# Decode attention with a cached K and V: K loaded through the DMA's transposing crossbar, V and weights moved to a second queue, scores laid out by key group

## The chip, the cores, the metric

One core of a Trainium2 chip (trn2). The metric is the device time of one execution, in microseconds (us). Most executions of a kernel agree within 0.3%; where a run fell in a slower state it is said. Engines: PE is TensorE, DVE is VectorE, ACT is ScalarE, POOL is GpSimd, SP is SyncE, which issues loads. PEld is TensorE's loading of weights, a q after an engine's name (SPq) is its instruction queue, and L488 is line 488 of the kernel. K and V are the cached keys and values; the two measuring kernels below ran once each, so their state is unknown.

## The reference, cut

Two identical layers, run one after the other on 4 batch rows with one token each. Each layer is grouped attention over a cache (32 query heads, 8 K/V heads, 4096 keys, head size 128), then a gated MLP (a GLU).

```python
def _A_ref(x, k_cache, v_cache, wq, wo):          # x: 4 x 1 x 512
    q = (x @ wq).reshape(B, 1, 32, 128).transpose(0, 2, 1, 3)
    k = repeat(k_cache, 4, axis=1)                # 4 x 8 x 4096 x 128 before repeat
    v = repeat(v_cache, 4, axis=1)
    p = softmax(einsum("bhqd,bhkd->bhqk", q, k) * 128 ** -0.5)
    return einsum("bhqk,bhkd->bhqd", p, v)... @ wo
# reference: x += A(norm(x)); x += B(norm(x)); and both once more, same weights, same caches
```

Both layers use the same K and V. The kernel reads K once for a row and keeps it until layer 2 has used it, and reads V twice: 32 MiB of K, 64 MiB of V, 13.25 MiB of weights.

## The kernel before

A small planner in the kernel gives each operation an engine and an order, and gives each K or V tile one of the slots of a ring in SBUF. Everything is loaded by SyncE, in one order. A tile is half of a K or V head (512 KiB), and the ring has 22 slots. K arrives as it lies in memory, keys on partitions; VectorE turns it in 32 x 32 blocks of pairs, in place.

```python
    NS = 22                                        # ring slots of 512 KiB
    ...
    def load_piece(src, q):
        t = _Tile(src)
        def fn(e):
            return e.dma_start(
                ring[t.slot], t.src.rearrange("(p t) d -> p (t d)", p=P)[:, q * TS:(q + 1) * TS])
        S.load(t, fn, P * TS * 2)                  # SyncE's queue
        return t
    ...
    def transpose_k(b, g, q, prio):                # VectorE, 64 times
            v = ring[t.slot].bitcast(dt.int32)
            return e.transpose(v, v)
    ...
    def scores(b, s, u, prio):                     # rows by head
            for nn in range(NQ):
                for gi in range(4):
                        kt = ring[t.slot].rearrange("p (t bb j r) -> p t bb j r", bb=2, j=32, r=2)
                        return e.matmul(
                            bank[32 * gi:32 * gi + 16, :], lhsT=qbd[u % NQB][:, gi, nn, :],
                            rhs=kt[:, :, nn // 2, :, nn % 2], start=nn == 0, stop=nn == NQ - 1)
    ...                                            # softmax; the probabilities are transposed twice
    # load order for row b: V (layer 2 of row b-1, heads 0..2), K(b), V (layer 1), V (layer 2 of b-1, heads 3..7)
```

The score matmuls read columns 4 bytes apart. A K slot is free only when layer 2's scores have read it, and these need the whole of layer 1 for that row.

## Time and profile before

| | before |
|---|---|
| median of 2 runs | 348.98 us (348.31 to 349.64) |
| span of the profiled run | 344.2 us |
| bytes moved | 115.3 MB, all but a little on one queue |
| TensorE / VectorE / ScalarE busy | 222.9 / 138.4 / 52.8 us |
| K transposes on VectorE | 64, 75.8 us |
| score matmuls | 512, four at a time in 0.43 us at half clock |

The page of the kernel before. The rows with 40 digits or numbers cut the span into 40 slices of 8.6 us: DMA is the busy share of the 16 DMA engines in tenths, GB/s what they moved. The last line is a DMA queue: packets, MB, share of the engines' time.

```profile
span 344.2 us, 11881 instructions
...
DMA  7999999999489999998599999957999999977800
GB/s 264 375 401 409 408 345 365 409 401 377 192 275 405 410 407 372 374 381 320 172 393 409 409 368 347 404 179 280 334 416 407 410 354 382 343 284 256 356 5 2
...
q1 hardware_dynamic: 36816, 114.57, 88.1%
```

In the slices in which nothing holds it up, the queue runs at 401 to 416 GB/s; at 410 GB/s the bytes are 281 us. The rest of the span is visible as low slices: 192, 172, 179 and the last two.

The chain of waits of the same kernel, by engine and then by line (share of the span):

```profile
DMA 40%; PE 27%; issue 14%; DVE 10%; SPq 7%; POOLq 0%; ACT 0%; DVEq 0%
DMA ring<-in_A_v_cache_dram 31%; PE S_ps L488 7%; PE O_ps L571 6%; PE M_ps L298 6%; PE Y_ps L298 5%; DMA wd<-in_B_w_down_dram 5%; SPq L331 5%; DVE ring L475 4%; DMA wo<-in_A_wo_dram 3%; PE G_ps L298 2%; SPq L347 2%; DVE ml L504 2%; DMA ring<-in_A_k_cache_dram 2%; PE PT_ps L298 1%; DVE qbd L466 1%
```

Loads lead; VectorE's K transposes (DVE ring) are 4% of it. In the costliest groups (columns: line, engine, operation, out<-in, shape, count | busy us, mean ns | idle before it and its main cause) they look much larger:

```profile
L571 PE MATMUL O_ps<-pt_sb,ring 128*128 128x4 bf16 x2048 | 67.2, 167 | 39.5 <-DMA ring<-in_A_v_cache_dram 31.6
...
L475 DVE STREAM_TRANSPOSE ring<-ring 128x1024 int32<-128x1024 int32 x64 | 75.8, 1216 | 8.6 <-DMA ring<-in_A_k_cache_dram 8.2
L488 PE MATMUL S_ps<-ring,qbd 128*16 128x512 bf16 x512 | 55.7, 590 | 12.0 <-DVE ring L475 12.0
```

75.8 us of work, of which 4% of the span stood in the way. One of the dips, in windows of 4 us (busy us of each engine with instruction counts, clock, DMA share, GB/s), and one undisturbed window:

```profile
core 0: us, PE busy (x) PEld busy (x) DVE busy (x) ACT busy (x) POOL busy (x), PEclk, DMA share, GB/s
160.00:164.00 4.00, 3.10 (x102) 2.99 (x101) 0.58 (x2) 0.18 (x1) 0.54 (x1) 0.50 0.70 271
164.00:168.00 4.00, 4.00 (x60) 1.48 (x60) 1.26 (x3) 0.18 (x1) 0.00 (x0) 0.50 0.24 67
...
256.00:260.00 4.00, 2.00 (x21) 0.43 (x18) 3.93 (x7) 0.00 (x0) 0.00 (x0) 0.50 1.03 414
```

At 164 us the DMA rate drops to 67 GB/s: the ring is full of K tiles that wait for the scores of layer 2. SyncE's waits show it: four times loads waited for a score matmul, once for 14 us:

```profile
engine line waited for: us in total, times, longest us
SPq L190 <- PE S_ps L488: 38.9, 4, 14.0
```

These scores, in order of time (start, duration, engine, line, operation, count):

```profile
164.02 1.89 PE L488 MATMUL S_ps<-ring,qbd 128*16 128x512 bf16 x16
```

16 matmuls of 512 columns in 1.89 us, four column groups at a time. By their starts, each four begin 0.43 us after the four before (the granted clock was half in this window, 0.50).

### The profile page before, as it was taken

Reading aid. Unit: us, or ns where it says so; the run is one execution under the profiler, and the core shown is the slowest. Engines: PE = TensorE matmul, PEld = TensorE weight load, DVE = VectorE, ACT = ScalarE, POOL = GpSimd, SP = SyncE. Lnnn points to the kernel's source line nnn. Section 1 sums busy time; section 2 is a strip of 40 time slices with the busy share of each in tenths; the row PEclk is TensorE's granted clock in tenths of the full one; section 3 lists DMA queues with packets and bytes.
Section 4 is the critical chain, followed back from the end, with each engine's and each line's share of the span. In section 5 each row is a group of like instructions: output and inputs, shape, how many; then the busy total and the mean of one; then the engine's idle time right before and its main releaser. Section 6 shows DMA issues by size and latency. Waiting matters only on the chain.

```text
span 344.2 us, 11881 instructions
## 1 busy us (share of the span) xinstructions
PE 222.9 (65%) x5426; PEld 171.2 (50%) x5426; DVE 138.4 (40%) x341; ACT 52.8 (15%) x128; POOL 10.6 (3%) x38
## 2 busy tenths in 40 slices
PE   1332861265877578676874697596784787777876
PEld 1202551155635147676352376493452586762865
DVE  3777620000189951101699620011899400016111
ACT  1003030000033203000241130000323110003300
POOL 6000000000000000000000000000000000000001
PEclk9999999999995555555655555555655555558555
DMA  7999999999489999998599999957999999977800
GB/s 264 375 401 409 408 345 365 409 401 377 192 275 405 410 407 372 374 381 320 172 393 409 409 368 347 404 179 280 334 416 407 410 354 382 343 284 256 356 5 2
DMA packets 36897, 115.32 MB, mean 335 GB/s; under 512 B 3312, under 2 KB 9200, under 8 KB 36848
## 3 DMA queue, kind: packets, MB, share of 16 engines
q1 hardware_dynamic: 36816, 114.57, 88.1%
q8 instruction: 42, 0.69, 0.8%
q14 instruction: 7, 0.06, 0.0%
q10 hardware_dynamic: 32, 0.00, 0.0%
HBM read 114.56 MB, written 0.00 MB: 333 GB/s over the span
## 4 chain that ended last, share of the span: by engine, by line
DMA 40%; PE 27%; issue 14%; DVE 10%; SPq 7%; POOLq 0%; ACT 0%; DVEq 0%
DMA ring<-in_A_v_cache_dram 31%; PE S_ps L488 7%; PE O_ps L571 6%; PE M_ps L298 6%; PE Y_ps L298 5%; DMA wd<-in_B_w_down_dram 5%; SPq L331 5%; DVE ring L475 4%; DMA wo<-in_A_wo_dram 3%; PE G_ps L298 2%; SPq L347 2%; DVE ml L504 2%; DMA ring<-in_A_k_cache_dram 2%; PE PT_ps L298 1%; DVE qbd L466 1%
## 5 line engine op out<-in xcount | busy, mean ns | idle before, releaser
L571 PE MATMUL O_ps<-pt_sb,ring 128*128 128x4 bf16 x2048 | 67.2, 167 | 39.5 <-DMA ring<-in_A_v_cache_dram 31.6
L571 PEld LDWEIGHTS O_ps<-pt_sb,ring 128*128 128x128 bf16 x2048 | 63.7, 105 | 48.0 <-DMA ring<-in_A_v_cache_dram 20.3
L475 DVE STREAM_TRANSPOSE ring<-ring 128x1024 int32<-128x1024 int32 x64 | 75.8, 1216 | 8.6 <-DMA ring<-in_A_k_cache_dram 8.2
L488 PE MATMUL S_ps<-ring,qbd 128*16 128x512 bf16 x512 | 55.7, 590 | 12.0 <-DVE ring L475 12.0
L528 ACT ACTIVATE p_sb<-S_ps,cols 128x512 bf16<-128x512 f32 x32 | 24.6, 773 | 92.3 <-DVE cols L523 92.3
L504 DVE TENSOR_REDUCE ml<-S_ps 128x1 f32<-128x512 f32 x32 | 21.6, 674 | 38.1 <-PE S_ps L488 38.1
L580 DVE TENSOR_TENSOR oT<-O_ps,winv 128x12 bf16<-128x12 f32 (+2 forms) x29 | 4.9, 169 | 68.9 <-PE O_ps L571 68.7
L488 PEld LDWEIGHTS S_ps<-ring,qbd 128*16 128x16 bf16 x512 | 13.5, 111 | 34.0 <-issue 17.6
L298 PE MATMUL Y_ps<-oT,wo 128*128 128x1 bf16 (+1 forms) x640 | 20.4, 166 | 9.2 <-DVE oT L580 5.7
L298 PEld LDWEIGHTS Y_ps<-oT,wo 128*128 128x128 bf16 x640 | 18.7, 104 | 11.5 <-DVE oT L580 7.0
L298 PE MATMUL PT_ps<-ident_b,p_sb 128*128 128x64 bf16 x128 | 11.0, 228 | 18.6 <-ACT p_sb L528 18.4
L298 PEld LDWEIGHTS PT_ps<-ident_b,p_sb 128*128 128x128 bf16 x128 | 7.0, 116 | 26.4 <-ACT p_sb L528 24.5
L298 PE MATMUL M_ps<-xT,wq 128*128 128x1 bf16 x512 | 15.4, 165 | 6.7 <-issue 4.1
L298 PEld LDWEIGHTS M_ps<-xT,wq 128*128 128x128 bf16 x512 | 14.5, 104 | 7.5 <-issue 4.3
L298 PE MATMUL M_ps<-dsel,cols 128*128 128x16 f32 x64 | 15.1, 355 | 2.7 <-DVE dsel L553 2.7
L437 POOL TENSOR_TENSOR cols<-cols 128x1 f32<-128x1 f32 (+1 forms) x10 | 6.4, 640 | 325.0 <-issue 217.4
L433 DVE TENSOR_SCALAR cols<-G_ps 128x1 f32<-128x1 f32 (+1 forms) x10 | 1.6, 158 | 35.7 <-PE G_ps L298 35.7
L298 PEld LDWEIGHTS M_ps<-dsel,cols 128*128 128x128 f32 x64 | 13.7, 298 | 3.4 <-DVE dsel L553 2.8
L426 ACT ACTIVATE gs<-xj,cols 128x4 f32<-128x4 f32 x8 | 2.4, 297 | 81.6 <-DVE cols L424 81.6
L547 ACT ACTIVATE pt_sb<-PT_ps 128x512 bf16<-128x512 f32 x16 | 9.6, 597 | 22.4 <-PE PT_ps L298 22.4
L298 PE MATMUL G_ps<-cols 128*128 128x1 f32 (+1 forms) x40 | 11.4, 354 | 2.4 <-DVE cols L403 0.9
L536 ACT ACTIVATE p_sb<-PT_ps 128x512 bf16<-128x512 f32 x16 | 9.6, 597 | 12.3 <-PE PT_ps L298 12.3
(73 smaller groups left out, 151.2 us busy)
## 6 DMA issues: line engine op xcount, KB each, us to landing
ring<-in_A_v_cache_dram SPq DMA_DIRECT2D x128, 512.0 KB, 7.5
ring<-in_A_k_cache_dram SPq DMA_DIRECT2D x64, 512.0 KB, 11.9
wq<-in_A_wq_dram SPq DMA_DIRECT2D x4, 1024.0 KB, 12.4
wo<-in_A_wo_dram SPq DMA_DIRECT2D x4, 1024.0 KB, 11.1
wg<-in_B_w_gate_dram SPq DMA_DIRECT2D x1, 1792.0 KB, 13.8
wu<-in_B_w_up_dram SPq DMA_DIRECT2D x1, 1792.0 KB, 11.8
wd<-in_B_w_down_dram SPq DMA_DIRECT2D x1, 1792.0 KB, 16.4
x<-in_A_x_dram SPq DMA_DIRECT2D x1, 4.0 KB, 1.6
```

Source lines behind the costliest of these rows:

```text
L298: return lambda e: e.matmul(o, lhsT=l, rhs=r, start=start, stop=stop)
L331: return e.dma_start(ring[t.slot], t.src.rearrange("(p t) d -> p (t d)", p=P)[:, q * TS:(q + 1) * TS])
L347: S.put("sp", lambda e: e.dma_start(o, i), 0.55, 0, writes=[key], dma=key, nbytes=nbytes)
L437: "pool", lambda e: e.tensor_tensor(rs, vpe[:, 0:nb], mhalf[:, 0:nb], ALU.pow), 0.6, prio,
L475: return e.transpose(v, v)
L488: return e.matmul(bank[32 * gi:32 * gi + 16, :], lhsT=qbd[u % NQB][:, gi, nn, :], rhs=kt[:, :, nn // 2, :, nn % 2], start=nn == 0, stop=nn ...
L504: "dve", lambda e, q=q: e.tensor_reduce(ml[:, q:q + 1], S_ps[banks[q]][:], AX.X, ALU.max, negate=True), 0.65,
L528: "act", lambda e, q=q: e.activation(p_sb[:, 4 * q:4 * q + 4, :].rearrange("p c x -> p (c x)"), S_ps[banks[q]][:], ACTF.Exp, bias=nbias, s ...
L536: "act", lambda e: e.activation(pt1.rearrange("p c g a h -> p (c g a h)"), PT_ps[:], ACTF.Copy), 0.65, prio,
L547: "act", lambda e: e.activation(pt_sb[pi][:].rearrange("p q c g h -> p (q c g h)"), PT_ps[:], ACTF.Copy), 0.65,
L571: return e.matmul(O_ps[:, gi * R:(gi + 1) * R], lhsT=ring[tile.slot][:, (t % HT) * DH:(t % HT + 1) * DH], rhs=pt_sb[pi][:, t % 4, t // 4, ...
L580: "dve", lambda e: e.tensor_tensor(o, O_ps[:, c0:c1], winv[pi][:, c0:c1], ALU.mult), 0.2, prio - 1.5,
```

## The change

Its intent: take the K transposes off VectorE by letting the DMA's crossbar turn K on its way in; with whole K heads turned, let each score matmul contract the full head size against a diagonal query block, with the rows of a score tile by key group instead of by head, which drops the spreading of q and the second transposition of the probabilities. Crossbar loads go on SyncE's queue, V and weights on GpSimd's. Tiles are whole heads (1 MiB) in 11 slots. The GLU's gate and up matmuls are split in four, so that a reciprocal root (rstd, GpSimd's power) runs under them. Core of the diff, cut:

```diff
-    NS = 22
+    NS = 11
@@ loads
-        def fn(e):
-            return e.dma_start(
-                ring[t.slot], t.src.rearrange("(p t) d -> p (t d)", p=P)[:, q * TS:(q + 1) * TS]
-            )
+    def load_k(b, g):
+        t = K[b, g] = _Tile(A_k[b, g])
+        S.load(t, "sp", lambda e, t=t: e.dma_start_transpose(ring[t.slot], t.src), P * TS * 2, 0.6, 3.9)
+    def load_v(l, b, g, parts=1):
+            S.load(
+                t, "pool", lambda e, t=t, i=i: e.dma_start(ring[t.slot][:, i * n:(i + 1) * n], t.src[:, i * n:(i + 1) * n]),
+                P * n * 2, 1.0,
+            )
-    def load_w(key, o, i, nbytes):
+    def load_w(key, o, i, nbytes, eng="pool"):
@@ scores: no transposes on VectorE
-                            bank[32 * gi:32 * gi + 16, :], lhsT=qbd[u % NQB][:, gi, nn, :],
-                            rhs=kt[:, :, nn // 2, :, nn % 2], start=nn == 0, stop=nn == NQ - 1,
+                            S_ps[u % 2][32 * j:32 * j + 16, q, :], lhsT=qd[:, 16 * g:16 * g + 16],
+                            rhs=ring[t.slot].rearrange("d (p t) -> d t p", t=T)[:, t0:t0 + 4, :],
+                            start=g == 0, stop=g == 3,
@@ GLU: gate and up in four pieces each, rstd after the second
+            for f0, f1 in ((0, 3), (3, 6), (6, 10), (10, NF)):
```

The number 3.9 is the planner's own: it takes SyncE as blocked for 3.9 us by each crossbar load of 1 MiB, and plans the bytes at the plain rate. V needs keys by `(p t)`, so the scores must read K's columns `t` apart: 32 columns, 64 bytes.

## The prediction

> **What bounds the kernel now.** The loads. The page counts 115.3 MB in a span of 344.2 us. In undisturbed slices (the page's second part) the queue moves 405 to 411 GB/s; at 410 the bytes alone are 281 us. The other 63 us are gaps. By the table of 4 us windows: the start (4 us), the tail after the last load (324 to 344, 19 us), one dip per batch row, near 86-100, 160-172, 222-244 and 296-316 (about 9, 10, 14, 10 us); the rest is scattered. Each dip is one dependency: K tiles hold their ring slots until layer 2's scores have read them, which needs the whole chain last V tile, output projection, GLU, q projection, q spread, scores. In row 1 it ran from about 144 to 166 us (timeline). From one layer-2 score to the next (93.0, 164.0, 237.4, about 309) it is some 72 us, of which a row's 24 MiB are 61.4 us at 410 GB/s. VectorE's K transposes are 75.8 us busy (64 of 1.2 us), but only 3.6% (12 us) of the chain of waits: mostly hidden behind loads.
>
> **Removed.** The stream transposes; q spread (16 small matmuls and 0.43 us on VectorE per unit); the second transposition of the probabilities (16 matmuls, a 0.60 us ACT copy). Scores keep 512 matmuls of 512 columns (0.43 us per four in the cold clock), but start, and release, per K tile. On the dip's chain I count 2 to 3 us saved per row, some 10 us in all; in the first stage, where 84.5 us were used for bytes worth 75, 4 to 5 us.
>
> **Added.** (a) K through the crossbar. The new planner itself blocks SyncE 3.9 us per MiB (269 GB/s) and fills the rest with V, 2:1, so 8 K + 4 V take 31.2 us against 30.8 for plain loads: free, if the crossbar doesn't also use up the engines. The Trainium skill (DMA: Bandwidth & Descriptors, "Latency and other measured facts") gives 261 GB/s for a bad layout, about 350-400 for a contiguous one; K is contiguous. Estimate from that page: at 350, 32 MiB cost 14 us more; at 261 with nothing beside it, over 40. No trace here shows it yet. (b) GpSimd's queue also holds the rstd powers of the chain (0.54 us each): loads wait behind them and they behind loads. (c) A ring of 11 slots of 1 MiB leaves three, not six, for V while K is held, and less cover (7 MiB, not 8): 1 to 3 us per row. (d) Scores read K at a 64-byte stride; the skill (Advanced Engine Details and Errata, "Memory Cachelines") says changing the line at every access costs. At the half clock I expect little.
>
> **Sum.** 349 - 5 (start) - 10 (chain) - 6 (less VectorE and PE work in the V stages) + 7 (transposition, mostly filled) + 0 to 5 (GpSimd, ring) = 335 to 340. I predict 337 us, 80% range 316 to 364; faster 0.57, same 0.21, slower 0.22.
>
> **Checks.** Right: VectorE busy near 60 us; K tiles landing every 3.9 us while total GB/s stays near 400; one dip per row, 2 to 3 us shorter; period 67 to 70 us. Wrong: 270-330 GB/s throughout the K stages with engines full (crossbar-bound, slower); GpSimd's power waiting on loads; scores clearly above 0.43 us per four; V stages below 380 GB/s with PE waiting for V (three slots too few).

## The result, and the profile after

458.32 us (458.16 to 458.47, 2 runs) against 348.98 us: 31% slower, ratio 1.313 (1.302 to 1.324). A ratio here and below is the mean time of one kernel's fast runs over that of the other's of the same rounds, so not quite the ratio of the medians that are quoted. The predicted 337 us and its range of 316 to 364 missed it widely.

The page of the changed kernel, slices of 11.4 us:

```profile
span 456.0 us, 10567 instructions
...
DMA  8999978999999795999799995999799969985800
GB/s 252 370 311 243 230 161 333 323 366 307 192 292 262 123 226 199 373 366 228 195 302 211 239 76 195 382 360 220 202 328 212 276 122 405 358 303 201 357 4 2
...
q0 software_dynamic: 13120, 81.01, 49.6%
q1 hardware_dynamic: 132128, 33.56, 45.0%
```

The engines are busy nearly all the time (DMA row) and yet many slices move only 120 to 250 GB/s, and one 76. K's queue (q1) moved 33.56 MB in 132128 packets, 254 bytes each, and took 45% of the engines' time; V's and the weights' (q0) moved 81 MB in 13120 packets in 49.6%. Before, all 114.57 MB needed 36816 packets.

The chain of waits:

```profile
PE 32%; DMA 30%; SPq 20%; issue 13%; DVE 2%; ACT 1%; POOL 1%; DVEq 0%; ACTq 0%; POOLq 0%
SPq L315 19%; DMA ring<-in_A_v_cache_dram 13%; PE S_ps L443 12%; DMA ring<-in_A_k_cache_dram 12%; PE O_ps L509 6%; DMA wd<-in_B_w_down_dram 6%; PE M_ps L286 5%; PE Y_ps L286 5%; PE G_ps L286 3%; ACT p_sb L471 1%; DVE cols L457 1%; PE S_ps L286 1%; POOL ring L322 0%; POOL wo L327 0%; DVE oT L518 0%
```

SPq L315 is SyncE's sequencer at the line that issues the crossbar loads: 19% of the span it is held there. Score matmuls (L443) are 12%. The groups:

```profile
L443 PE MATMUL S_ps<-ring,q1d 128*16 128x512 bf16 x256 | 59.7, 1025 | 90.9 <-DMA ring<-in_A_k_cache_dram 86.8
...
L443 PE MATMUL S_ps<-ring,q2d 128*16 128x512 bf16 x256 | 57.2, 1031 | 0.4 <-issue 0.4
```

The score matmuls take 1025 ns each where they took 590, 116.9 us in all instead of 55.7, and those of layer 1 wait 86.8 us for K. In order of time, 48 of layer 2's in one go:

```profile
218.10 10.45 PE L443 MATMUL S_ps<-ring,q2d 128*16 128x512 bf16 x48
```

48 in 10.45 us are 0.87 us for four, where it was 0.43. Windows of 4 us (columns as before) in the K stage of the third row:

```profile
256.00:260.00 4.00, 0.00 (x0) 0.00 (x0) 0.00 (x0) 0.00 (x0) 0.00 (x0) 0.50 1.29 258
260.00:264.00 4.00, 0.00 (x0) 0.00 (x0) 0.00 (x0) 0.00 (x0) 0.00 (x0) 0.50 1.32 57
264.00:268.00 4.00, 0.00 (x0) 0.00 (x0) 0.00 (x0) 0.00 (x0) 0.00 (x0) 0.50 1.31 43
268.00:272.00 4.00, 1.28 (x8) 0.11 (x8) 0.00 (x0) 0.00 (x0) 0.00 (x0) 0.50 1.25 38
```

This is the strangest thing in the trace: from 260 to 272 us the DMA engines count as more than fully busy and move 38 to 57 GB/s. The trace's packet records show whose time this is. K's queue alone makes 1.19 to 1.25 of the busy share: its 256-byte packets took 283 to 321 ns each on average, where they took 18 from 240 to 244 us, with no V under way. V's packets of 8 KiB took 312 to 314 ns (their median in the whole run is 309), but only 11 to 20 of them went in 4 us. SyncE's crossbar loads (columns: duration of the issue, min/median/max):

```profile
engine op xcount: duration ns min/median/max, first and last start us, forms
L315 SPq DMA_TRANSPOSE ring<-in_A_k_cache_dram x32: 3881/5082/30418, 1.2 to 350.7; - x32
```

An issue takes 3.9 us at best, as the planner thought, 5.1 us typically and 30 us at worst. From one layer-2 score to the next it is 101, 104 and 91 us, where it was 71.0, 73.4 and 71.0.

VectorE did what was meant: 54.6 us busy instead of 138.4.

### The profile page after: what moved, and what is told of

It is laid out like the page before. It is cut to its first block, busy times and chain, and to the rows that moved or that the text cites. A ratio compares the mean times of both kernels' runs of the same rounds, so it can differ in the third digit from the quotient of the medians.

```text
span 456.0 us, 10567 instructions
## 1 busy us (share of the span) xinstructions
PE 275.9 (61%) x4946; PEld 162.6 (36%) x4946; DVE 54.6 (12%) x200; ACT 40.3 (9%) x112; POOL 55.6 (12%) x104
## 3 DMA queue, kind: packets, MB, share of 16 engines
q0 software_dynamic: 13120, 81.01, 49.6%
q1 hardware_dynamic: 132128, 33.56, 45.0%
## 4 chain that ended last, share of the span: by engine, by line
PE 32%; DMA 30%; SPq 20%; issue 13%; DVE 2%; ACT 1%; POOL 1%; DVEq 0%; ACTq 0%; POOLq 0%
SPq L315 19%; DMA ring<-in_A_v_cache_dram 13%; PE S_ps L443 12%; DMA ring<-in_A_k_cache_dram 12%; PE O_ps L509 6%; DMA wd<-in_B_w_down_dram 6%; PE M_ps L286 5%; PE Y_ps L286 5%; PE G_ps L286 3%; ACT p_sb L471 1%; DVE cols L457 1%; PE S_ps L286 1%; POOL ring L322 0%; POOL wo L327 0%; DVE oT L518 0%
## 5 line engine op out<-in xcount | busy, mean ns | idle before, releaser
L443 PE MATMUL S_ps<-ring,q1d 128*16 128x512 bf16 x256 | 59.7, 1025 | 90.9 <-DMA ring<-in_A_k_cache_dram 86.8
L509 PE MATMUL O_ps<-pt_sb,ring 128*128 128x4 bf16 x2048 | 64.5, 166 | 41.2 <-DMA ring<-in_A_v_cache_dram 28.3
L322 POOL DMA_DIRECT2D ring<-in_A_v_cache_dram x69 | 37.0, 537 | 328.5 <-PE O_ps L509 212.1
L443 PE MATMUL S_ps<-ring,q2d 128*16 128x512 bf16 x256 | 57.2, 1031 | 0.4 <-issue 0.4
L443 PEld LDWEIGHTS S_ps<-ring,q1d 128*16 128x16 bf16 x256 | 4.0, 89 | 109.0 <-DMA ring<-in_A_k_cache_dram 79.0
L457 DVE TENSOR_REDUCE cols<-S_ps 128x1 f32<-128x1024 f32 x16 | 19.6, 1225 | 177.6 <-PE S_ps L443 177.6
L443 PEld LDWEIGHTS S_ps<-ring,q2d 128*16 128x16 bf16 x256 | 6.5, 103 | 36.9 <-issue 36.8
L286 PEld LDWEIGHTS M_ps<-cols,same 128*128 128x128 f32 x32 | 7.2, 281 | 23.7 <-issue 20.5
L286 PEld LDWEIGHTS S_ps<-ident_b,p_sb 128*128 128x128 bf16 x128 | 6.4, 113 | 17.5 <-issue 12.0
L286 PE MATMUL G_ps<-cols 128*128 128x1 f32 (+1 forms) x40 | 11.4, 354 | 1.6 <-DVE cols L378 0.9
L286 PE MATMUL M_ps<-cols,same 128*128 128x4 f32 x32 | 8.6, 338 | 4.5 <-DVE cols L461 2.8
```

The source lines that it names most:

```text
L286: return lambda e: e.matmul(o, lhsT=l, rhs=r, start=start, stop=stop)
L322: t, "pool", lambda e, t=t, i=i: e.dma_start(ring[t.slot][:, i * n:(i + 1) * n], t.src[:, i * n:(i + 1) * n]),
L443: return e.matmul(S_ps[u % 2][32 * j:32 * j + 16, q, :], lhsT=qd[:, 16 * g:16 * g + 16], rhs=ring[t.slot].rearrange("d (p t) -> d t p", t= ...
L457: "dve", lambda e: e.tensor_reduce(ml, sp_[:].rearrange("p q x -> p (q x)"), AX.X, ALU.max, negate=True), 1.2,
L509: return e.matmul(O_ps[:, gi * R:(gi + 1) * R], lhsT=ring[tile.slot][:, t * DH:(t + 1) * DH], rhs=pt_sb[pi][:, t // 16, t % 4, t // 4 % 4, ...
```

## The experiments

Theory A: the crossbar costs. Its loads use up the DMA engines (they aren't filled by V for free), and beside another queue they starve. Rival B: the score matmuls cost, which read columns 64 bytes apart. Rival C: the second queue and the ring of 11 slots cost by themselves. Many of these kernels compute wrong scores on purpose. Their outputs passed the comparison with the reference all the same, so this comparison isn't sensitive to the scores.

The runs went to several chips; the kernel before, run again beside each group, had medians of 348.4 to 349.3 us, so times can be compared across them.

### Plain K loads in the changed kernel (e1_plain_k)

```diff
-        S.load(t, "sp", lambda e, t=t: e.dma_start_transpose(ring[t.slot], t.src), P * TS * 2, 0.6, 3.9)
+        S.load(t, "sp", lambda e, t=t: e.dma_start(ring[t.slot], t.src.rearrange("(p t) d -> p (t d)", p=P)), P * TS * 2, 0.6, 3.9)
```

> The changed kernel with the 32 K loads as plain loads on the same queue, same order, same waits (wrong scores on purpose). Theory A (the crossbar loads are what costs: 256-byte packets, 3.9 us per MiB at best, and far less while V loads run beside them): falls from 458 us by 60 to 90 us, to 370-400 us; total rate in the K stages back near 400 GB/s. Rival B (the 64-byte stride of the score reads costs most): falls by less than 30 us. Rival C (GpSimd's queue and the ring of 11 slots): falls by less than 30 us, V stages stay as they are.

Measured: 389.99 us (388.63 to 391.35), 68 us less. Theory A is a large part, but not all.

### Neighbouring columns (e2_contig)

```diff
-                            rhs=ring[t.slot].rearrange("d (p t) -> d t p", t=T)[:, t0:t0 + 4, :],
+                            rhs=ring[t.slot][:, t0 * P:(t0 + 4) * P],
```

> The changed kernel with the score matmuls reading 512 neighbouring columns instead of columns 64 bytes apart (wrong scores on purpose), crossbar loads kept. Theory B (stride): score matmuls fall from 1.9 us to near 0.95 us per eight, PE busy falls by about 57 us, and the time by 30 to 60 us. Theory A: the matmuls get faster all the same, but the time falls by less than 25 us, because the K tiles arrive late anyway.

Measured: one fast run of 433.96 us, one slow one of 443.01 (the profiled one). Against 458 it is 24 us by the fast run alone, so the number is soft. In the slow run's profile the two groups of score matmuls were 56.6 us busy instead of 116.9, and layer 1's waited 127.0 us for K instead of 86.8: most of what the matmuls gained they then waited for K. That is what theory A expects of B's cure, but a slow run can only hint at it; the fast runs e5 and e12 below show it on one queue.

### Both (e3_both)

> The changed kernel with both: plain K loads and neighbouring columns (wrong scores on purpose). If A and B together are the whole loss, it lands at 325 to 345 us, at or below the kernel before. If GpSimd's queue and the ring of 11 slots of 1 MiB (C) cost too, it stays above 355 us.

Measured: 356.69 us (356.23 to 357.15), ratio to before 1.021 (1.012 to 1.031). The two together are 102 us. What is left is 8 us above the kernel before, so a third cost is at work, or the gains that I had predicted aren't there (the verdict at 2% is unclear).

### The loads and the reads by themselves (m1_bench)

A kernel that only loads and then only multiplies; for a stage, e.g.:

```python
phases = [("plain", None, None), ("xbar", None, None), ("plain", 8192, "pool"), ("xbar", 8192, "pool"),
          ("xbar", 8192, "act"), ("xbar", 1024, "pool"), ("xbar", 8192, "sp")]   # K kind, V's row bytes, V's issuer
# 8 K loads of 1 MiB on SyncE, 8 V loads of 1 MiB where a second entry is given; all waited for between stages
```

> A kernel that only measures (wrong output on purpose). Seven stages of DMA, each of 8 K loads of 1 MiB, separated by waits: plain alone, crossbar alone, plain beside 8 V loads from GpSimd's queue, crossbar beside them, crossbar beside V from ScalarE's queue, crossbar beside V in rows of 1 KiB, crossbar and V in turn on SyncE's queue. Then score-like matmuls with columns 2, 4, 8, 16, 32 and 64 bytes apart. Theory A: crossbar alone 230 to 290 GB/s against 400 plain; beside V of another queue K moves one 256-byte packet for each 4 KB packet of V, under 40 GB/s, until V is through, so 16 MiB take about 41 + 30 us, the same from ScalarE's queue; with 1 KiB rows K gets a fairer share; on one queue no starving. Theory B: groups of four matmuls stay at 0.22 us (full clock) or 0.43 us (half clock) up to 8 or 16 bytes and about double at 32 and 64 bytes. If instead the 1.9 us per eight came from the DMA writes beside them, all strides read the same here.

The windows of this kernel, one for each stage in that order:

```profile
core 0: us, PE busy (x) PEld busy (x) DVE busy (x) POOL busy (x), PEclk, DMA share, GB/s
2.20:24.50 22.30, 0.00 (x0) 0.00 (x0) 2.96 (x1) 0.00 (x0) 1.00 0.92 376
24.50:59.30 34.80, 0.00 (x0) 0.00 (x0) 0.00 (x0) 0.00 (x0) 1.00 1.11 241
59.30:101.40 42.10, 0.00 (x0) 0.00 (x0) 0.00 (x0) 4.36 (x8) 1.00 0.97 399
101.40:157.20 55.80, 0.00 (x0) 0.00 (x0) 0.00 (x0) 4.16 (x8) 1.00 1.09 301
157.20:216.00 58.80, 0.00 (x0) 0.00 (x0) 0.00 (x0) 0.00 (x0) 1.00 1.05 285
216.00:283.00 67.00, 0.00 (x0) 0.00 (x0) 0.00 (x0) 7.03 (x8) 1.00 1.07 261
283.00:340.00 57.00, 0.00 (x0) 0.00 (x0) 0.00 (x0) 0.00 (x0) 1.00 1.07 283
```

Stage 2: the crossbar alone fills the engines and moves 241 GB/s in the whole stage, and 242 to 264 GB/s by the packet records in 4 us steps, which is some 4.1 us for 1 MiB; plain loads take 2.56 us at 410 GB/s. SyncE's eight issues of this stage took 3.8 to 4.2 us each, with nothing beside them: about as long as the engines need for the data. Stage 4 takes 55.8 us where 8 x 4.1 + 8 x 2.56 is 53: nothing is filled, the two add up. The packet records of stage 4 show how: from 108 to 124 us, while V was under way, V moved 397 to 410 GB/s and K 13 to 15, in 256-byte packets against packets of 8 KiB; when V was through, K went back to about 255. From ScalarE's queue (stage 5) it was the same, K 12 to 14 GB/s from 164 to 180 us, so it isn't GpSimd's doing alone. In turn on one queue (stage 7) it took 57.0 us, and nobody starved. Expected were packets of 4 KB for V; they were of 8 KiB. V in rows of 1 KiB (stage 6) went in packets of 4 KiB, half as large, and K's share rose to 22 GB/s beside 328 of V (226 to 242 us). The stage as a whole took 67.0 us, 14 more than the sum; why, I haven't tested.

The Trainium skill (DMA: Bandwidth & Descriptors, "Queues, rings and completion order") says that each DMA engine takes turns between queues a packet at a time. The records agree, in number too: in 4 us, stage 4 moved 210 to 229 packets of K and 194 to 200 of V, stage 6 some 340 and 320. One for one, a K packet is a 32nd of V's 8 KiB (12 to 13 GB/s beside 400) and a sixteenth of its 4 KiB (some 20 beside 328). So in these stages the size of the other queue's packets set K's share.

Then the matmuls, at full clock throughout. The start times of the weight loads of four matmuls show the pace, two lines each at columns 8, 16 and 64 bytes apart (first column start, second duration; a stage is 32 such groups, so where it lies follows from adding up the paces):

```profile
358.29 0.19 PEld L110 LDWEIGHTS stride<-mv,wt 128*16 128x16 bf16 x4 [0.28 <-issue]
358.75 0.19 PEld L110 LDWEIGHTS stride<-mv,wt 128*16 128x16 bf16 x4 [0.27 <-issue]
...
373.66 0.19 PEld L110 LDWEIGHTS stride<-mv,wt 128*16 128x16 bf16 x4 [0.71 <-issue]
374.56 0.19 PEld L110 LDWEIGHTS stride<-mv,wt 128*16 128x16 bf16 x4 [0.71 <-issue]
...
441.15 0.18 PEld L110 LDWEIGHTS stride<-mv,wt 128*16 128x16 bf16 x4 [0.68 <-issue]
442.01 0.18 PEld L110 LDWEIGHTS stride<-mv,wt 128*16 128x16 bf16 x4 [0.68 <-issue]
```

0.46 us for four at 8 bytes, 0.90 at 16, 0.86 at 64 (0.92 at 32). At 2 and 4 bytes it was 0.22 (46 groups in 10 us). So a 64-byte step costs four times at full clock, and in the kernel, at half clock, 0.87 against 0.43: the slow reads don't care about the clock. The changed kernel shows this by itself. Layer 2's first 48 score matmuls of the first row ran at a granted clock of 1.00, and took as long as the 48 at 218 us above, most of which ran at 0.50:

```profile
116.71 10.45 PE L443 MATMUL S_ps<-ring,q2d 128*16 128x512 bf16 x48
```

No DMA ran beside the measuring kernel's matmuls, so the reads themselves are slow. The skill (Advanced Engine Details and Errata, "Memory Cachelines") says that two accesses in a 16-byte line are enough for full rate. The direction agrees; the threshold doesn't, for 8 bytes apart was already half as fast.

### One queue for everything, K plain, neighbouring columns (e4_one_queue)

```diff
-                t, "pool", lambda e, t=t, i=i: e.dma_start(ring[t.slot]...
+                t, "sp", lambda e, t=t, i=i: e.dma_start(ring[t.slot]...
-    def load_w(key, o, i, nbytes, eng="pool"):
+    def load_w(key, o, i, nbytes, eng="sp"):
```

> The run with plain K loads and neighbouring columns (356.7 us) again, but with V and the weights issued by SyncE too, in one order with K (wrong scores on purpose). If GpSimd's queue (its issue times, its rstd powers waiting among the loads, two queues sharing the engines) makes the 8 us that this variant has over the kernel before, it falls to 346-350 us. If the ring of 11 slots of 1 MiB makes them, it stays at 354-360 us.

Measured: 335.51 us (334.27 to 336.06), ratio to before 0.962 (0.956 to 0.968). That is 21 us less than on two queues, and lower than either outcome that I had written down, for I hadn't allowed for the gains of the rest. This kernel has everything that the change was meant to bring and none of the three costs. It has one thing more, which the prediction didn't count: plain loads of 1 MiB go in packets of 8 KiB, those of 512 KiB before in packets of 4 KiB, and the undisturbed slices run at 420 to 424 GB/s, not 401 to 416. At 422 instead of 410 GB/s, 115 MB take some 8 us less (an estimate), so not all of the 14 us to the kernel before need be gains that I had predicted. Its page, slices of 8.3 us:

```profile
GB/s 262 403 420 422 368 409 369 359 400 376 284 249 421 422 413 392 373 365 286 224 420 423 421 386 358 390 381 178 410 424 420 399 360 383 349 277 209 409 20 4
```

It computes wrong scores, so it is a measure and not a kernel to use.

### One queue, with the crossbar and the 64-byte reads (e5_xbar_one_queue)

This is the changed kernel with only the queue of V and weights changed, as above.

> The changed kernel with V and the weights issued by SyncE too, in one order with the crossbar loads (results as they should be). The measuring kernel says that crossbar and plain loads then add up (4.1 and 2.6 us per MiB) and nobody starves. Starving beside another queue is a cost of its own: the time falls from 458 us to 415-440. If the crossbar's use of the engines is all of its cost: within 8 us of 458. It could even rise, if SyncE's blocking while it issues a crossbar load delays V.

Measured: 404.87 us (404.59 to 405.15), 53 us less than on two queues. So the second queue is a cost of its own beside the crossbar's use of the engines. Its page, slices of 10.1 us:

```profile
DMA  7999999999999999999799999997999999958400
GB/s 279 279 261 240 247 399 412 349 398 289 250 246 250 244 361 380 414 328 255 159 275 264 271 402 367 372 227 214 270 243 278 356 377 369 366 217 334 189 3 4
```

The slices of the K stages (240 to 280) now run at the crossbar's rate, and the slices of 76 and 123 GB/s are gone. Still, the engines are full in the K stages and move 250.

### The reverse, in the kernel before: crossbar alone (e7_before_xbar)

```diff
+            if kk:
+                return e.dma_start_transpose(ring[t.slot], t.src[q * TS:(q + 1) * TS, :])
```

> The kernel before with each K half tile loaded through the crossbar, everything else kept, VectorE's transposes too (wrong scores on purpose). One queue, so no starving. Additive theory: 32 MiB at 4.1 instead of 2.56 us per MiB, 49 us more where nothing is idle, less what falls into the dips: 385 to 400 us. If the crossbar were filled for free by V, under 360 us.

Measured: 421.55 us (421.22 to 421.89), 72 us more than before, above the range. Here K comes in 64 loads of 512 KiB, and several of its K slices run at 193 to 235 GB/s, below even the crossbar's own rate. Why, I haven't tested.

### The reverse: stride alone (e8_before_stride)

```diff
-                        kt = ring[t.slot].rearrange("p (t bb j r) -> p t bb j r", bb=2, j=32, r=2)
+                        kt = ring[t.slot].rearrange("p (x s) -> p s x", s=32)
-                            rhs=kt[:, :, nn // 2, :, nn % 2], start=nn == 0, stop=nn == NQ - 1,
+                            rhs=kt[:, 8 * nn:8 * nn + 8, :], start=nn == 0, stop=nn == NQ - 1,
```

> The kernel before with its score matmuls reading columns 64 bytes apart instead of 4 (wrong scores on purpose). Score matmuls go from 0.43 to about 0.95 us per four, PE busy rises by about 55 us. About half lies on the path from q to the freed K slots (two units per row, some 7 us per row) or holds up V: the time rises by 15 to 35 us. If under 7 us, the stride costs only in combination with the late K of the change.

Measured: 393.79 us (390.84 to 396.42), 44 us more. From its groups:

```profile
L488 PE MATMUL S_ps<-ring,qbd 128*16 128x512 bf16 x512 | 119.6, 1075 | 10.8 <-DVE ring L475 10.8
```

This group is busy 64 us longer (PE as a whole 56), and the time rises by some 44: more than I expected. In the chain of waits these matmuls are 25% of the span, where they were 7%.

### Stride alone, crossbar alone, on one queue (e11_one_queue_stride, e12_one_queue_xbar)

> All loads on SyncE's queue, K plain, and the 64-byte reads of the change back (wrong scores on purpose). Against the same with neighbouring columns (335.5 us) it is the stride alone: on two queues the stride was worth 33 us, in the kernel before 44 us; here 25 to 45 us, so 360 to 380 us. If stride and the crossbar hide each other on one queue, this and the next run add up to more than the 69 us that both cost together.

> All loads on SyncE's queue, K through the crossbar, neighbouring columns (wrong scores on purpose). Against 335.5 us it is the crossbar alone, without another queue beside it: additive theory, 32 MiB at 4.1 instead of 2.56 us per MiB = 49 us, so 378 to 392 us. If above 400, the crossbar also costs something that isn't engine time (its issue blocks SyncE).

Measured: 369.85 us (368.18 to 371.51) and 399.58 us (399.45 to 399.70). With these, all eight combinations have been run:

| medians, us | plain K, neighbouring | plain K, 64 bytes | crossbar, neighbouring | crossbar, 64 bytes |
|---|---|---|---|---|
| all on SyncE's queue | 335.5 | 369.9 | 399.6 | 404.9 |
| V and weights on GpSimd's queue | 356.7 | 390.0 | 434.0 (one fast run) | 458.3 (the change) |

The stride alone costs 34 us and the crossbar alone 64, but both together 69: while K comes at the crossbar's pace, TensorE has time for slow reads. The traces of the two crossbar runs on one queue, both fast, agree: with neighbouring columns layer 1's scores waited 62.3 us for K, with the 64-byte reads 22.1. The second queue costs 21 us without crossbar and stride, 20 with the stride, 34 with the crossbar (by the one fast run) and 53 with both.

### Is it GpSimd or the second queue? (e13_one_queue_pool)

All loads on GpSimd, K too, with its powers among them.

> All loads, K plain, neighbouring columns, as in the run of 335.5 us, but all issued by GpSimd, with the rstd powers among them (wrong scores on purpose). If the 21 us between one and two queues come from two queues sharing the engines (V gets only half the rate while K runs ahead of its need): 333 to 341 us. If they come from GpSimd itself (its issue, loads and powers waiting for one another): 350 to 360 us.

Measured: 340.45 us (338.87 to 342.26). GpSimd as the issuer costs 5 us; the other 16 of the 21 come with two queues. One thing differs beside the queues: the plans of the two-queue runs with plain K still block SyncE 3.9 us for each K load, those of the one-queue runs with plain K don't. What this is worth hasn't been tested. What two queues do is visible in the third stage of the measuring kernel: plain K and plain V share evenly, 195 to 227 GB/s each in the packet records. In the two-queue run itself it was the same from 108 to 128 us, 176 to 240 GB/s each. So I take it that K, asked for ahead of its need, halves the rate of the V tile that TensorE waits for, where one queue keeps the planner's order; the two runs show the size of it and not this cause.

### Does two-queue traffic lose rate or only order? (m2_bench)

```python
phases = [("xbar", 1, False), ("xbar", 2, False), ("xbar", 2, True), ("plain", 1, False), ("plain", 2, False)]
# 8 K loads on SyncE; 6 V loads on GpSimd, of which so many in flight; True: they start after the first K has landed
```

> A kernel that only measures (wrong output on purpose). Five stages of 8 K loads of 1 MiB on SyncE's queue beside 6 V loads from GpSimd's: crossbar with one V in flight (each waits for the one before), crossbar with two, crossbar with two that start after the first K has landed, plain with one, plain with two. Adding up: crossbar stages 8 x 4.1 + 6 x 2.56 = 48 us, plain stages about 36 us. If only the order is lost, the crossbar stages take 48 to 53 us and the total rate never falls under 230 GB/s while both have work. If both slow each other down, they take over 60 us, with stretches well under 150 GB/s.

The windows: the three crossbar stages, then three steps of 4 us inside the second.

```profile
2.40:52.90 50.50, 0.00 (x0) 0.00 (x0) 2.76 (x1) 2.65 (x5) 1.00 1.12 291
52.90:127.00 74.10, 0.00 (x0) 0.00 (x0) 0.00 (x0) 3.17 (x6) 1.00 1.14 198
127.00:186.80 59.80, 0.00 (x0) 0.00 (x0) 0.00 (x0) 3.16 (x6) 1.00 1.10 246
76.00:80.00 4.00, 0.00 (x0) 0.00 (x0) 0.00 (x0) 0.00 (x0) 1.00 1.25 87
80.00:84.00 4.00, 0.00 (x0) 0.00 (x0) 0.00 (x0) 0.00 (x0) 1.00 1.27 50
84.00:88.00 4.00, 0.00 (x0) 0.00 (x0) 0.00 (x0) 0.67 (x2) 1.00 1.24 74
```

With one V in flight the stage takes 50.5 us, as the sum says. With two it takes 74.1, and from 76 to 88 us both queues together move 50 to 87 GB/s with full engines: the stretches of the changed kernel's trace, made anew. Here too it is K's packets of 256 bytes that fill the engines' time, with 88 to 183 ns each on average against 18 or so alone. The third stage, also with two in flight, took 59.8. With plain K beside two V loads the two queues lost nothing: that stage took 37.4 us, at 423 GB/s while both had work. (With one V in flight the plain stage took 46.2 us instead of the 36 that I expected: K was through after 29 us, and the last V loads went one at a time.) So beside the crossbar it isn't only the order: at times crossbar loads and V loads of another queue slow each other down, to between a fifth and a third of what the crossbar moves alone. When this happens, and why not in m1's stage with eight in flight, is open. The trace doesn't say which of the 16 engines moved a packet.

### Is it a stale plan? (e15_xbar_replanned)

```diff
-        S.load(t, "sp", ..., P * TS * 2, 0.6, 3.9)
+        S.load(t, "sp", ..., int(P * TS * 2 * 1.6), 0.6, 3.9)
```

> The run with all loads on SyncE's queue, K through the crossbar and neighbouring columns (399.6 us), but the planner counts a crossbar load as 1.6 times its bytes, so that slots and order are planned for the rate that was measured (wrong scores on purpose). If a stale plan makes the 15 us over the additive 49: 384 to 392 us. If not: 396 to 403 us.

Measured: 396.26 us (393.46 to 399.06) against 399.58. The plan isn't it. Of the crossbar's 64 us on one queue, 49 are its rate (32 x (4.1 - 2.56)); the other 12 to 15 stay open. (By the 422 GB/s of this kernel's plain loads it would be 52, and 9 to 12 stay open.)

### The ring alone, in the kernel before (e9_before_ring11)

22 slots of 512 KiB become 11 of 1 MiB, with one load each.

> The kernel before with the ring of the change: 11 slots of 1 MiB, one load for a whole K or V tile, everything else kept (correct). My prediction put 1 to 3 us per row on the coarser ring: 352 to 358 us. If the ring costs nothing: 345 to 351 us.

Measured: 346.71 us (344.61 to 348.27), ratio 0.997 (0.990 to 1.004). All in all the coarser ring costs nothing. But this run too has the packets of 8 KiB, with undisturbed slices at 418 to 425 GB/s, so a small cost of the ring may hide behind the faster loads; no run parts the two.

### One part of the change that pays, in the kernel before (e10_before_split)

```diff
-            for f in range(NF):
-                for k in range(KD):
-                    ...
-            S.put("pe", fns, 1.85, prio, reads=[xtkey, key], writes=[bkey])
-            if w is wg:
-                rstd(4.0, rs, "rs_h", nb, prio)
+            for f0, f1 in ((0, 3), (3, 6), (6, 10), (10, NF)):
+                ...
+                if w is wg and f1 == 6:
+                    rstd(4.0, rs, "rs_h", nb, prio)
```

> The kernel before with one small part of the change: the GLU's gate and up matmuls in four pieces, so that the rstd (two engines' hops and GpSimd's power) runs under them (correct). By the traces the chain gets about 1 to 1.5 us shorter in each of four rows and at the end: 342 to 348 us against 349; if the dips are then covered by V loads anyway, no difference.

Measured: 343.39 us (340.87 to 345.60), ratio 0.986 (0.980 to 0.991). It computes what the reference asks for. That is 1.4% less than before: the interval leaves out 1, but the verdict at 2% is unclear.

Two attempts didn't build and weren't run: a crossbar load that also reorders the keys, so that the scores could read neighbours and be right, and the rstd power on VectorE.

## Why the prediction was wrong

The sum was 349 - 5 - 10 - 6 + 7 + 0 to 5. Term by term:

| term of the prediction | predicted | measured |
|---|---|---|
| start | -5 us | about 0: the first layer-2 scores start at 92.5 us in the one-queue plain run, 93.0 before |
| dip chain | -10 us | -8 us: from one layer-2 score to the next 69.1 us on average against 71.8, three times |
| V stages, less work | -6 us | about -2 us, in the tail: 33.4 us from the last row's layer-2 scores to the end, 35.8 before; in the rows it can't be parted from the line above |
| crossbar | +7 us | +64 us alone on one queue |
| 64-byte reads | "little" | +34 us alone and +5 beside the crossbar, on one queue; some +24 beside the crossbar on two (one fast run) |
| GpSimd's queue and the ring | 0 to +5 us | ring 0, larger packets included; the second queue +21 us, and +53 beside the crossbar and the 64-byte reads |

About half of the gains were there, some 11 us of the 21 by the first three lines: a kernel with all of them and none of the three costs ran at 335.5 us. That they came the way I said isn't shown, for the packets of 8 KiB alone could save up to some 8 us. The step that failed first is "so 8 K + 4 V take 31.2 us against 30.8 for plain loads: free, if the crossbar doesn't also use up the engines". It does: the crossbar alone held the engines full at about 255 GB/s, and loads beside it added up. So the term "+ 7 (transposition, mostly filled)" was 64 us on one queue. I had read the planner's 3.9 us as time in which SyncE issues and the engines are free, because the sum came out so well; it was the engines' own pace, seen from SyncE: with nothing beside them, the issues took 3.8 to 4.2 us, and the data 4.1. I wrote down the case ("at 261 with nothing beside it, over 40") and then gave it little weight. The range should have held it.

The second wrong step is "Scores read K at a 64-byte stride [...] At the half clock I expect little". The slow read takes about 0.9 us for four matmuls whatever the clock, so at half clock it is still twice the time. It is worth 34 us by itself and 5 beside the crossbar on one queue. In the change itself undoing it gave 24 us, by the one fast run: it is not where most of the 109 us went.

The third is "loads wait behind them and they behind loads": I looked for the second queue's cost in GpSimd's own order, and that is 5 us. The cost came with the second queue, 16 us more without the crossbar, probably because a share by packets replaces the planned order. Beside the crossbar the share is 256 bytes against 8 KiB, and both at times slow each other down. So the way from 335.5 to 458.3 is: +69 for crossbar and stride on one queue, +53 for the second queue beside them. The costs don't add up, so another order of undoing them gives other shares. Shown are these sizes, the packet share and the mutual slowing in a kernel by itself; not shown is the mechanism of the slowing, nor how the 53 us divide between share and slowing, nor the last 9 to 15 us of the crossbar.

Of the signs that I had named, two of the wrong side came true: full engines in the K stages, at rates below even the 270 to 330 GB/s that I had named, and scores far above 0.43 us for four. VectorE came near 60 us busy (54.6), which says that the removal worked and nothing about the time.

## What to carry to other kernels

When a change moves work from an engine that waits on loads to the loads themselves, measure the loads' rate alone and beside the others first: one small kernel with stages between waits told here what a planner's constant had hidden. If loads bound the kernel and a plan relies on their order, try one queue first: here the second cost 21 us, and 53 beside packets of 256 bytes. And ask of any new layout what the matmul's moving operand then reads: here, a step of 64 bytes took twice the time at half clock, and steps of 16 bytes or more four times at full.

## What the Trainium skill lacked or had wrong

- Advanced Engine Details and Errata, "X-Bar Transpose (TRN2)": says that transposing loads are as fast as others, 350-400 GB/s expected. Here 1 MiB of contiguous 256-byte rows went at 241 GB/s over a stage (about 255 steady) with full engines and nothing beside it. DMA: Bandwidth & Descriptors, "Latency and other measured facts", gives 261 GB/s for a layout that isn't contiguous; this one is contiguous and no faster.
- DMA: Bandwidth & Descriptors, "Rules for kernel authors": says that a transpose next to ordinary DMAs needs nothing. For correctness no run here contradicts it (but the comparison isn't sensitive to the scores); for time they do: K fell to 12 to 15 GB/s beside V of another queue, and with two V loads in flight a stage worth 48 us took 74.1, with stretches of 50 to 87 GB/s.
- The same page, "Rules for kernel authors", says that spreading loads over issuing engines doesn't raise bandwidth. No page says that it can cost: 356.7 us on two queues against 335.5 on one (340.5 all on GpSimd).
- Advanced Engine Details and Errata, "Memory Cachelines": two hits in a 16-byte line are said to be enough. Four concurrent matmuls at full clock took 0.22 us at 4 bytes apart, 0.46 at 8, 0.90 at 16, about the same at 32 and 64. The page doesn't say that the slow rate is independent of the TensorE clock (48 matmuls took 10.45 us at clock 1.00, and the same mostly at 0.50).
